# RetNet recurrence and quick-GELU block on one core: decays on GpSimd, four weight loads on GpSimd's queue, keys of step 1 ahead of a weight half, and outputs copied earlier

## The chip, the cores and the metric

The kernel runs on one core of a Trainium2 chip. The metric is the device time of one launch in microseconds (us). A core has five engines that run side by side: PE (matrix products; its weight loads are listed as PEld), DVE (vector), ACT (activation functions and copies), POOL (GpSimd) and SP, which here only issues DMA transfers. Each engine works through its own list of instructions in order, and waits at an instruction until the semaphores it names have been raised by other engines or by transfers that have landed.

## The reference

```python
# attention: q, k, v are (4 batches, 8 heads, 768 positions, 64)
for t in range(S):
    state = gamma * state + k[:, :, t] (outer) v[:, :, t]
    y[:, :, t] = scale * q[:, :, t] @ state
x = y.transpose(0, 2, 1, 3).reshape(3072, 512)
# feed-forward, w_in (512, 2048), w_out (2048, 512)
h = x @ w_in
g = h * (1 / (1 + exp(-1.702 * h)))
out = g @ w_out
```

The attention has one gamma per head and is a recurrence over positions. All inputs but the weights are float32; the two weight matrices reach the kernel as 64-bit floats, that is as pairs of 32-bit words.

## The kernel before, in words

**Attention in steps.** The recurrence is done in chunks of 64 positions, for two batches at a time: 24 steps, numbered j or f. For a step PE turns the queries and keys (`turn_new`, L283), multiplies them within the chunk (`scores`, L339), adds to the state (`gain`, L347), applies the old state (`past`, L358) and the chunk's own scores (`own`, L367). DVE masks the scores (`masked`, L380), scales the share of the old state by the row's decay (`by_state`, "state" in the list, L387), adds both shares into X (`output`, "x" in the list, L409) and adds the gain to the state (`updated`, L432). For step 0 there is no old state, and `output` is a plain copy out of PSUM on ACT (L300, the helper `copy`). `decay` multiplies a step's keys by their column decays: on GpSimd as one instruction over the tile (L318), on ACT as eight instructions, one for each head (L323). `aged` multiplies the state by the decay of a whole chunk (L418 on DVE, L421 on ACT, L423 on POOL).

Scores and gain share one PSUM tile, PAS; past and own share another, PYS. The scores of the next step wait until the state update that reads PAS is done, and past waits until the output copy of the step before has read PYS.

**Weights.** Each pair of 64-bit pieces is fetched by a DMA of 512 KB (`fetch`, L201; `w0a`, `w0b` and so on) into one of three raw places (RAWS: two in W2 and one in G, taken in the order RING), and is narrowed to float32 by six instructions of the class `Narrow`: `abs` (ACT, L237), `low` (ACT, L241), `clip` (DVE, L245), `lift` (DVE, L248), `sign` (DVE, L253), `rest` (DVE, L258). A raw place is free for the next pair when `low` and `sign` of the pair in it are done. Pairs 4 and 7 go to raw places 1 and 2, after pairs 1 and 5.

**Feed-forward.** While weights still arrive, PE multiplies the finished half pieces (`up0` and `up1`, "up" in the list, L476), ACT applies the GELU (`hidden`, "gate", L457), and later units use a product scheme with seven instead of eight products (`zero`, L559, and `seven`, L599), whose sums of weights (`seven_4`, `seven_6`, `seven_52`) and of inputs (`zero_x`, L546) DVE makes. From about 148 us on the down products and the other blocks follow (L954, L698, L821), with the remaining attention steps placed between them.

**What sets the order.** Everything of the first two blocks of four steps is named in one list, written out by hand, at the end of the kernel function. The loop below it calls the works in that order, and their instructions are pinned to it on each engine; `name@engine` gives the engine. So the place of a name in the list sets the place of its instructions in the queue of every engine it uses, and for a load its place in the queue of SP, ACT or POOL:

```python
    for name in """
        row@sp k0@act table q0 v0 z5 rows ...
    """.split():
        name, *e = name.split("@")
        works[name](*[{"sp": sp, "pool": pool, "act": act, "dve": dve}[x] for x in e])
```

A few instructions of `halves_anew` ("anew") are not pinned, and the scheduler places them on POOL: a copy that rewrites `cold` (L1048; it waits until the last decay on ACT has read it), the load of `whole_h` (L1045) and a copy of the mask (L1047).

SP's and ACT's transfers, and POOL's, wait before issue for one of eight landing semaphores of their kind, taken in turn: the ninth transfer waits for the first to land. For steps below 6 the keys come once, by four transfers of 64 KB, and are turned by PE. From step 6 on queries and keys come in squares of 32 (`load`, L176, eight transfers of 32 KB each) that DVE transposes (L294), and the keys come a second time in rows (kn, L161).

Of the kernel before, what the change touches and what calls it, by code (L numbers as in the profile page):

```python
# [28 lines left out]
def kernel(  # L29
# [29 lines left out]
    pe, act, dve, pool, sp = nc.tensor, nc.scalar, nc.vector, nc.gpsimd, nc.sync  # L59
# [42 lines left out]
    rowd = const.tile([P, HP, D], F32, name="rowd")  # L102
    row = G[0:1, 4, 0:2].rearrange("p a (h t) -> p (a h) t", t=D)
    ones = G[0:1, 4, 2, 0:P]
    cold = const.tile([P, 2 * H], F32, name="cold")
    whole = const.tile([P, HP], F32, name="whole")
# [3 lines left out]
    mask = const.tile([P, 2, HP, D], F32, name="mask")  # L110
# [32 lines left out]
    def load(j, what="qkv", engine=None):  # L143

        b, c = j // NC * 2, j % NC
        rows = slice(c * D, (c + 1) * D)
        keep = send if j < 2 * CB else lambda i: i

        def plain(name, src, tag, bufs, engine=sp):
            t = two.tile([P, H, D], F32, name=name + "_in", tag=tag, bufs=bufs)
            QKV[name, j] = t
            for i in range(2):
                if j < NEW:
                    to, at = t[i * D:(i + 1) * D], src[b + i, :, rows, :].rearrange("h p d -> p h d")
                    for n in range(1 if name == "v" else 2):
                        keep(engine.dma_start(*((to, at) if name == "v" else (to[:, n:H:2], at[:, n * HP:(n + 1) * HP]))))
                else:
                    for r in range(2):  # L160
                        keep(engine.dma_start(t[r * D:(r + 1) * D, i * HP:(i + 1) * HP],  # L161
                                              src[b + i, r * HP:(r + 1) * HP, rows, :].rearrange("h p d -> p h d")))

        if j < NEW:
            if "q" in what:
                QKV["q", j] = t = two.tile([P, H * D], F32, name="q_in", tag="q_sq", bufs=2)
                keep((engine or sp).dma_start(t, q[b:b + 2, :, rows, :].rearrange("i h (k p) d -> (i h) k (p d)", p=8)))
            if "k" in what:
                plain("kn", k, "k_sq" if j in (0, 1, 4, 5) else "o", 2, engine or pool)
        elif "q" in what:  # L170
            for name, src in (("q", q), ("k", k)):
                t = two.tile([P, H, D // C4, C4], F32, name=name + "_sq")
                for r0 in range(0, P, C4):
                    for n in range(D // C4):
                        t0 = c * D + n * C4
                        tc.keep_in_program_order(sp.dma_start(  # L176
                            t[r0:r0 + C4, :, n], src[b + r0 // D, :, t0:t0 + C4, r0 % D:r0 % D + C4]
                            .rearrange("h p d -> p h d")))
                QKV[name, j] = t
        if "v" in what:  # L180
            if j >= NEW and c < NC - 1:
                plain("kn", k, "kn", 1)
            plain("v", v, "v", 2, engine or sp)
# [102 lines left out]
    def turn(j):  # L286

        if j < NEW:
            turn_new(j, 1)
            turn_new(j, 0)  # L290
        else:
            QT[j], KT[j] = home(j, "qT"), home(j, "kT")
            for t, name in ((QT[j], "q"), (KT[j], "k")):
                tc.keep_in_program_order(dve.transpose(  # L294
                    t.rearrange("p h t -> p (h t)"), QKV.pop((name, j)).rearrange("p h n d -> p (h n d)")))
        if 2 * CB <= j < NCH - 2:
            load(j + 2, "qk")
# [136 lines left out]
    def step(j, f=None):  # L434
        attend(j, f)
        if j is not None:
            masked(j)
            if j > 2 * CB:
                decay(j)
        if f is not None:  # L440
            c = f % NC
            if c == 0:
                updated(f)
            else:
                by_state(f)
            output(f)
            if 0 < c < NC - 1:
                aged(f)
                updated(f)
        if j is not None and 2 * CB < j < NCH - 1:  # L450
            load(j + 1, "v")
# [587 lines left out]
    def late_loads():  # L1039
        load(2 * CB, "qkv")  # L1040
        load(2 * CB + 1, "qk")
# [61 lines left out]

    begin()
    for name in """
        row@sp k0@act table q0 v0 z5 rows turn_q0 turn_k0 q1 w0b k1@sp w0a mask causal turned_q0
        turned2_q0@dve turned_k0 decay0@pool score0 v1 turn_k1 turn_q1 masked0 gain0 turned_k1 turned_q1 turned2_q1@dve own0 abs0b low0b updated0
        decay1@pool score1 clip0b lift0b sign0b rowd whole q2 k2@sp masked1 abs0a low0a rest0b x0 past1 gain1
        clip0a lift0a sign0a own1 rest0a aged1 turn_k2 turn_q2 w2b w2a state1 updated1 x1 turned_k2 turned_q2 turned2_q2@dve
        v2 q3 k3@sp up0.0.2 score2 abs2 decay2 aged2@dve q4 clip2 lift2 sign2 low2 decay3 w3b w3a  # L1110
        masked2 turn_k3 turn_q3 k4@sp gain2 past2 own2 v3 q5 rest2 k5@sp gate0.0.2 turned_k3 turned_q3 turned2_q3@dve updated2
        state2 score3 decay4 low3 turn_q4 turn_k4 up0.0.3 x2 masked3 gain3 past3 own3 abs3 clip3 lift3 sign3
        turned_q4 turned2_q4@dve rest3 turned_k4 score4 turn_k5 turn_q5 up0.0.6 w1a w5b w1b aged3 updated3 state3 w5a v4
        x3 up0.1.3 turned_q5 turned2_q5@dve gate0.0.3 abs1 low1 abs5 clip1 aged4 lift1 sign1 masked4 own4 gain4 w6a
        rest1 clip5 lift5 gate0.0.6 sign5 up0.0.7 past4 w6b decay5 low5 rest5 updated4 v5 gain5 w4a abs6
        gate0.1.3 turned_k5 clip6 state4 x4 lift6 score5 masked5 w4b abs4 up0.1.7 low6 aged5 gate0.0.7 w7a w7b
        low7 low4 q6 sign6 v6 own5 rest6 past5 seven_4.2 state5 gate0.1.7 seven_6.2 updated5 zero2.0 clip4 up0.1.6
        lift4 sign4 x5 seven_52.2 rest4 turn6 anew decay6 abs7 aged6 up0.1.2 w8a gate0.1.2 clip7 zero_x zero2.1
        score6 past6 q7 w8b v7 zero2.2 masked6 lift7 sign7 gain6 rest7 own6 w11b zero2.3 zero2.4 turn7
        w9a updated6 aged7 gate0.1.6 zero2.5 decay7 zero2.6 state6 w11a seven_4.0 x6 zero0.0 score7 masked7 abs8 clip8  # L1120
        past7 zero0.1 state7 seven_6.0 seven_52.0 lift8 sign8 gain7 own7 x7 seven_x zero0.2 zero0.3 zero0.4 zero0.5 low8
        seven_keep.2 w9b abs9 low11 clip9 rest8 lift9 zero0.6 w10a seven2.0 w10b seven2.1 abs11 clip11 lift11 sign11
        seven_4.1 rest11 seven2.2 abs10 seven2.3 seven2.4 seven_w.1 clip10 lift10 sign9 seven0.0 seven2.5 low10 low9 rest9 sign10
        updated7 rest10 seven_4.3 seven2.6 seven0.1 seven0.2 seven0.3 seven0.4 seven1.0 seven_keep.0 w14b w14a w12b w12a abs12 seven_w.3
        clip12 seven0.5 seven0.6 seven_v.1 lift12 sign12 abs14 clip14 low12 rest12 lift14 sign14 seven1.1 seven1.2 w13a seven1.3
        w13b abs13 low14 seven_v.3 clip13 lift13 seven1.4 sign13 seven3.0 seven1.5 rest14 seven1.6 seven3.1 seven3.2 seven3.3 seven3.4
        w15a seven_keep.3 seven_keep.1 w15b abs15 clip15 lift15 low13 low15 sign15 seven3.5 rest13 seven3.6 rest15 late_loads
    """.split():
        name, *e = name.split("@")
        works[name](*[{"sp": sp, "pool": pool, "act": act, "dve": dve}[x] for x in e])  # L1130
# [109 lines left out]
```

## Time and profile before

| what | value |
|---|---|
| median of the three runs | 650.57 us (649.11, 650.57, 650.80) |
| the profiled execution, its own time | 651.44 us |
| its span, first to last instruction | 649.7 us |
| PE busy | 633.4 us, 97% of the span |
| DVE busy | 435.6 us, 67% |
| ACT busy | 184.4 us, 28% |
| POOL busy | 152.0 us, 23% |
| mean granted clock of PE | 0.997 |
| DMA | 96.86 MB, mean 149 GB/s |
| line with most of PE's time | L821, 840 matmuls of one kind in 100.3 us, 276 ns each |

The page's rows give for a group of instructions the busy time, the mean of one, and the idle time of the engine just before them with what ended it. A row of the timeline gives the start in us from the first instruction, the length, the engine, the line, what is written and read, how many equal instructions are merged, and in brackets the idle time before it and its releaser. Rows of SPq, ACTq and the DMA rows of POOL are issues: the length is that of the issue and not of the transfer.

The profiled execution is one run, and its own time stands 0.87 us above the median; costs are worked out inside it.

### The profile page before, as it was taken

How to read it: one execution, taken by the hardware profiler on the slowest of the kernel's cores; microseconds unless marked ns; L12 is line 12 of the kernel's file. 1: busy time of each engine (PE TensorE's matmuls, PEld its weight loads, DVE VectorE, ACT ScalarE, POOL GpSimd, SP SyncE). 2: the span in 40 equal slices, each digit the busy share in tenths (PEclk: the TensorE clock that was granted, in tenths of full speed). 3: DMA queues.
4: the chain of work that ended last, by engine and by line, in shares of the span. 5: the costliest groups of instructions: out<-in, count | busy, mean ns of one | idle time of the engine just before them, and what ended most of it. 6: DMA issues, size and time to landing. Idle time of an engine off the chain costs nothing.

```text
span 649.7 us, 15510 instructions
## 1 busy us (share of the span) xinstructions
PE 633.4 (97%) x6543; PEld 578.4 (89%) x6543; DVE 435.6 (67%) x643; ACT 184.4 (28%) x329; POOL 152.0 (23%) x184
## 2 busy tenths in 40 slices
PE   7899999999999998999999999999999999999997
PEld 4788888888889997889999889999888999888997
DVE  2879887979989962438874337985246976145854
ACT  3778237661001102332101333100333110233210
POOL 4000211300612435000645000635300425200000
PEclk9989999999999999999999999999999999999999
DMA  9995587783368875720667730667741354221143
GB/s 198 228 258 161 112 252 214 198 209 57 93 200 264 206 175 171 200 67 4 172 179 213 215 85 1 160 161 189 211 95 49 89 174 143 110 91 49 59 153 98
DMA packets 150710, 96.86 MB, mean 149 GB/s; under 512 B 130512, under 2 KB 135888, under 8 KB 149616
## 3 DMA queue, kind: packets, MB, share of 16 engines
q1 hardware_dynamic: 138048, 42.83, 30.2%
q0 software_dynamic: 8672, 40.00, 19.3%
q10 hardware_dynamic: 3920, 13.04, 5.4%
q8 instruction: 51, 0.84, 0.6%
q14 instruction: 19, 0.16, 0.1%
HBM read 79.18 MB, written 14.94 MB: 145 GB/s over the span
## 4 chain that ended last, share of the span: by engine, by line
PE 83%; DMA 9%; SPq 5%; issue 1%; DVE 1%; ACT 1%; ACTq 0%
PE pq L821 33%; PE px L698 17%; PE pz L698 9%; PE pd L954 7%; PE ph L599 6%; PE py L698 4%; DMA W<-in_moe_w_out_dram 2%; SPq L161 2%; PE pa L339 2%; DMA q_in<-in_q_dram 2%; DMA kn_in<-in_k_dram 2%; DMA LATE<-W1D 1%; SPq L176 1%; PE py L367 1%; PE pa L347 1%; DMA v_in<-in_v_dram 1%
## 5 line engine op out<-in xcount | busy, mean ns | idle before, releaser
L821 PE MATMUL pq<-W,G 128*128 128x128 f32 x840 | 100.3, 276 | 0.0
L821 PEld LDWEIGHTS pq<-W,G 128*128 128x128 f32 x840 | 97.0, 192 | 0.8
L796 POOL DMA_DIRECT2D LATE<-W2D x34 | 18.7, 551 | 260.5 <-PE pq L821 139.8
L821 PE MATMUL pq<-LATE 128*128 128x128 f32 x560 | 74.8, 277 | 0.0
L821 PEld LDWEIGHTS pq<-LATE 128*128 128x128 f32 x560 | 68.2, 192 | 0.6
L698 PE MATMUL px<-X,LATE 128*128 128x256 f32 x256 | 60.6, 380 | 2.2 <-DMA LATE<-W1D 2.2
L698 PE MATMUL px<-X,W1A 128*128 128x256 f32 x256 | 60.5, 379 | 0.0
L698 PEld LDWEIGHTS px<-X,LATE 128*128 128x128 f32 x256 | 48.6, 190 | 9.1 <-issue 2.6
L698 PEld LDWEIGHTS px<-X,W1A 128*128 128x128 f32 x256 | 48.4, 190 | 6.3
L743 DVE TENSOR_TENSOR G<-pz,vv 128x512 f32<-128x512 f32 x16 | 11.1, 692 | 51.5 <-ACT vv L713 51.5
L843 ACT ACTIVATE o<-pq 128x512 f32<-128x512 f32 (+1 forms) x18 | 9.8, 544 | 119.9 <-PE pq L821 94.3
L457 ACT ACTIVATE G<-G 128x512 f32<-128x512 f32 x49 | 30.9, 630 | 43.1 <-DVE G L753 19.7
L821 PE MATMUL pq<-LATE,G 128*128 128x128 f32 x280 | 37.0, 275 | 0.0
L821 PE MATMUL pq<-W,LATE 128*128 128x128 f32 x280 | 37.0, 275 | 0.0
L954 PE MATMUL pd<-W,LATE 128*128 128x256 f32 x160 | 35.1, 380 | 0.0
L821 PEld LDWEIGHTS pq<-W,LATE 128*128 128x128 f32 x280 | 34.1, 192 | 0.0
L821 PEld LDWEIGHTS pq<-LATE,G 128*128 128x128 f32 x280 | 34.1, 192 | 0.0
L954 PEld LDWEIGHTS pd<-W,LATE 128*128 128x128 f32 x160 | 30.4, 190 | 4.1
L683 DVE TENSOR_TENSOR G<-G 128x512 f32<-128x512 f32 (+2 forms) x28 | 15.9, 567 | 23.5 <-ACT G L457 23.5
L810 DVE TENSOR_TENSOR LATE<-G 128x512 f32<-128x512 f32 x35 | 27.6, 789 | 5.0 <-PE pq L821 2.2
L476 PE MATMUL ph<-X,W1A 128*128 128x256 f32 x128 | 30.6, 397 | 0.2 <-DVE X L409 0.2
L698 PE MATMUL pz<-X,W1A 128*128 128x256 f32 x128 | 30.3, 380 | 0.0
(214 smaller groups left out, 1163.5 us busy)
## 6 DMA issues: line engine op xcount, KB each, us to landing
LATE<-W2D POOLq DMA_DIRECT2D x34, 768.0 KB, 5.2
W<-in_moe_w_out_dram SPq DMA_DIRECT2D x12, 512.0 KB, 6.0
LATE<-W1D ACTq DMA_DIRECT2D x4, 1536.0 KB, 9.7
LATE<-W1D POOLq DMA_DIRECT2D x4, 1536.0 KB, 8.9
kn_in<-in_k_dram SPq DMA_DIRECT2D x84, 64.0 KB, 4.8
W<-in_moe_w_in_dram SPq DMA_DIRECT2D x10, 512.0 KB, 4.8
out_dram<-o POOLq DMA_DIRECT2D x20, 256.0 KB, 4.6
q_sq<-in_q_dram SPq DMA_DIRECT2D x144, 32.0 KB, 3.0
```

The source lines that it names most:

```text
L161: keep(engine.dma_start(t[r * D:(r + 1) * D, i * HP:(i + 1) * HP], src[b + i, r * HP:(r + 1) * HP, rows, :].rearrange("h p d -> p h d")))
L339: pe.matmul(PAS[HALF[w], u, 0, s, :], kt[HALF[u], w, s, :], qt[HALF[u], w, s, :], start=True, stop=True)
L457: pin(act.activation(g, h[:, i], AF.Gelu_apprx_sigmoid))
L476: pe.matmul(h[:, ab], w, X[:, 2 * th + c // 2, c % 2, :], start=(ab == 0 and c == 0), stop=(c == 3), skip_group_check=True)
L599: pe.matmul(acc[:, u, :], w, x, start=(start and u == 0 and c == 0), stop=(stop and c == 1), skip_group_check=True)
L683: hold(dve.tensor_sub(q[0][1], q[0][0], q[0][1]))
L698: pe.matmul(acc[:, u, :], w1(2 * d + u, sw)[:, c, :], X[:, sx, c, :], start=(start and u == 0 and c == 0), stop=(stop and c == 1), skip_gr ...
L743: dve.tensor_add(a[3], z, v)
L796: engine.dma_start(c, W2D[i])
L810: dve.tensor_add(d[:, 0], s2, a11)
L821: pe.matmul(p0[:, j, :], a[:, d], w[:, d], start=(new and j == 0 and d == 0), stop=(d == NP // 2 - 1), skip_group_check=True)
L954: pe.matmul(p0[:, n, :], g1(m, p, sa)[:, n * P:(n + 1) * P], W2[:, sb, p, :], start=(new and p == 0 and n == 0), stop=(last and p == NP - ...
```

## The change

The list is edited in these places, and `load` lets queries and keys of the late kind be loaded apart:

- `k1@sp`, the four transfers of the keys of step 1, stands ahead of `w0b`, one of the two first weight halves, instead of behind it.
- `x0`, the plain copy of the outputs of step 0 on ACT, stands directly behind `score1` instead of behind `rest0b`; on ACT it passes the copies of the row decays and abs0a and low0a.
- `x1` stands ahead of `updated1`, so that two DVE instructions change places.
- `decay2` and `decay3` are done on POOL, by one instruction each, instead of on ACT by eight each.
- `w4a`, `w4b`, `w7a` and `w7b` are issued by POOL instead of SP.
- `q6` and the new `k6` (and `q7`, `k7`) load queries and keys apart. On SP the issues of q6, k6, the second keys and the values of step 6 keep their order among each other, but now nothing stands between v5 and them.

On POOL the unpinned instructions move too: the copy of `cold` stands between w4 and w7, and the load of `whole_h`, which was issued at 14.30 us, stands behind w7. PE's order does not change.

```diff
-        elif "q" in what:
-            for name, src in (("q", q), ("k", k)):
+        else:
+            for name, src in [(x, y) for x, y in (("q", q), ("k", k)) if x in what]:
...
-        row@sp k0@act table q0 v0 z5 rows turn_q0 turn_k0 q1 w0b k1@sp w0a mask causal turned_q0
+        row@sp k0@act table q0 v0 z5 rows turn_q0 turn_k0 q1 k1@sp w0b w0a mask causal turned_q0
...
-        decay1@pool score1 clip0b lift0b sign0b rowd whole q2 k2@sp masked1 abs0a low0a rest0b x0 past1 gain1
-        clip0a lift0a sign0a own1 rest0a aged1 turn_k2 turn_q2 w2b w2a state1 updated1 x1 turned_k2 turned_q2 turned2_q2@dve
-        v2 q3 k3@sp up0.0.2 score2 abs2 decay2 aged2@dve q4 clip2 lift2 sign2 low2 decay3 w3b w3a
+        decay1@pool score1 x0 clip0b lift0b sign0b rowd whole q2 k2@sp masked1 abs0a low0a rest0b past1 gain1
+        clip0a lift0a sign0a own1 rest0a aged1 turn_k2 turn_q2 w2b w2a state1 x1 updated1 turned_k2 turned_q2 turned2_q2@dve
+        v2 q3 k3@sp up0.0.2 score2 abs2 decay2@pool aged2@dve q4 clip2 lift2 sign2 low2 decay3@pool w3b w3a
...
-        rest1 clip5 lift5 gate0.0.6 sign5 up0.0.7 past4 w6b decay5 low5 rest5 updated4 v5 gain5 w4a abs6
-        gate0.1.3 turned_k5 clip6 state4 x4 lift6 score5 masked5 w4b abs4 up0.1.7 low6 aged5 gate0.0.7 w7a w7b
-        low7 low4 q6 sign6 v6 own5 rest6 past5 seven_4.2 state5 gate0.1.7 seven_6.2 updated5 zero2.0 clip4 up0.1.6
+        rest1 clip5 lift5 gate0.0.6 sign5 up0.0.7 past4 w6b decay5 low5 rest5 updated4 v5 q6 gain5 w4a@pool
+        abs6 gate0.1.3 turned_k5 clip6 state4 x4 lift6 score5 masked5 w4b@pool k6 abs4 up0.1.7 low6 aged5 gate0.0.7
+        w7a@pool w7b@pool low7 low4 sign6 v6 own5 rest6 past5 seven_4.2 state5 gate0.1.7 seven_6.2 updated5 zero2.0 clip4
...
-        score6 past6 q7 w8b v7 zero2.2 masked6 lift7 sign7 gain6 rest7 own6 w11b zero2.3 zero2.4 turn7
+        zero2.1 score6 past6 q7 k7 w8b v7 zero2.2 masked6 lift7 sign7 gain6 rest7 own6 w11b zero2.3
```

(The last lines of the list are only broken elsewhere.)

More of the change, by code (lines that the diff above doesn't have):

```diff
@@ L1114 @@
         x3 up0.1.3 turned_q5 turned2_q5@dve gate0.0.3 abs1 low1 abs5 clip1 aged4 lift1 sign1 masked4 own4 gain4 w6a
-        rest1 clip5 lift5 gate0.0.6 sign5 up0.0.7 past4 w6b decay5 low5 rest5 updated4 v5 gain5 w4a abs6
-        gate0.1.3 turned_k5 clip6 state4 x4 lift6 score5 masked5 w4b abs4 up0.1.7 low6 aged5 gate0.0.7 w7a w7b
-        low7 low4 q6 sign6 v6 own5 rest6 past5 seven_4.2 state5 gate0.1.7 seven_6.2 updated5 zero2.0 clip4 up0.1.6
-        lift4 sign4 x5 seven_52.2 rest4 turn6 anew decay6 abs7 aged6 up0.1.2 w8a gate0.1.2 clip7 zero_x zero2.1
@@ L1119 @@
-        score6 past6 q7 w8b v7 zero2.2 masked6 lift7 sign7 gain6 rest7 own6 w11b zero2.3 zero2.4 turn7
[L1120 to L1127, printed above, removed]
+        rest1 clip5 lift5 gate0.0.6 sign5 up0.0.7 past4 w6b decay5 low5 rest5 updated4 v5 q6 gain5 w4a@pool
@@ new lines @@
+        abs6 gate0.1.3 turned_k5 clip6 state4 x4 lift6 score5 masked5 w4b@pool k6 abs4 up0.1.7 low6 aged5 gate0.0.7
+        w7a@pool w7b@pool low7 low4 sign6 v6 own5 rest6 past5 seven_4.2 state5 gate0.1.7 seven_6.2 updated5 zero2.0 clip4
+        up0.1.6 lift4 sign4 x5 seven_52.2 rest4 turn6 anew decay6 abs7 aged6 up0.1.2 w8a gate0.1.2 clip7 zero_x
+        zero2.1 score6 past6 q7 k7 w8b v7 zero2.2 masked6 lift7 sign7 gain6 rest7 own6 w11b zero2.3
+        zero2.4 turn7 w9a updated6 aged7 gate0.1.6 zero2.5 decay7 zero2.6 state6 w11a seven_4.0 x6 zero0.0 score7 masked7
@@ new lines @@
+        abs8 clip8 past7 zero0.1 state7 seven_6.0 seven_52.0 lift8 sign8 gain7 own7 x7 seven_x zero0.2 zero0.3 zero0.4
+        zero0.5 low8 seven_keep.2 w9b abs9 low11 clip9 rest8 lift9 zero0.6 w10a seven2.0 w10b seven2.1 abs11 clip11
+        lift11 sign11 seven_4.1 rest11 seven2.2 abs10 seven2.3 seven2.4 seven_w.1 clip10 lift10 sign9 seven0.0 seven2.5 low10 low9
+        rest9 sign10 updated7 rest10 seven_4.3 seven2.6 seven0.1 seven0.2 seven0.3 seven0.4 seven1.0 seven_keep.0 w14b w14a w12b w12a
@@ L1128 @@
+        abs12 seven_w.3 clip12 seven0.5 seven0.6 seven_v.1 lift12 sign12 abs14 clip14 low12 rest12 lift14 sign14 seven1.1 seven1.2
+        w13a seven1.3 w13b abs13 low14 seven_v.3 clip13 lift13 seven1.4 sign13 seven3.0 seven1.5 rest14 seven1.6 seven3.1 seven3.2
+        seven3.3 seven3.4 w15a seven_keep.3 seven_keep.1 w15b abs15 clip15 lift15 low13 low15 sign15 seven3.5 rest13 seven3.6 rest15
+        late_loads
     """.split():
```

## The prediction

> **What bounds the kernel now.** I read the page, then the waits and the PE timeline of the first 110 us, then ACT, DVE, POOL and SP in the same stretch, the chain of waits, and the windows with the clock. The page first:
>
> ```profile
> span 649.7 us, 15510 instructions
> PE 633.4 (97%) x6543; PEld 578.4 (89%) x6543; DVE 435.6 (67%) x643; ACT 184.4 (28%) x329; POOL 152.0 (23%) x184
> ```
>
> PE idles for only 16.3 us of the span. By windows 9.1 us of that lies before 40 us, 1.3 us between 60 and 104 us, 5.2 us after 150 us. The change ends its moves by about 90 us, so what it can win is in the first two. The PE timeline of the start (start, length, what, idle before it and what ended it):
>
> ```profile
> 12.20 1.09 PE L283 MATMUL pt<-UB,kn_in 128*128 128x128 f32 x4 [1.38 <-DMA kn_in<-in_k_dram]
> 16.76 1.13 PE L339 MATMUL pa<-G 64*64 64x64 f32 x32 [0.71 <-DVE state L300]
> 18.84 1.13 PE L358 MATMUL py<-G,state 64*64 64x64 f32 x32 [0.95 <-ACT X L300]
> 23.76 4.16 PE L476 MATMUL ph<-X,W1A 128*128 128x256 f32 x16 [0.18 <-DVE X L409]
> 27.85 0.70 PE L339 MATMUL pa<-G 64*64 64x64 f32 x32
> 33.88 0.69 PE L339 MATMUL pa<-G 64*64 64x64 f32 x32 [2.72 <-ACT G L323]
> ```
>
> Two things are to be seen. PE waits in turn for the keys of step 1, for x0 (ACT) and, at 33.88, for the scores of step 3. And the same 32 matmuls take 1.13 us early and 0.70 us from 27.85 on: PE starts at half speed, though the clock column reads 1.00 there. ACT ahead of the 2.72 us hole:
>
> ```profile
> 25.47 2.01 ACT L323 ACTIVATE G<-kn_in,cold 128x64 f32<-128x64 f32 x8
> 27.38 1.18 ACT L241 ACTIVATE W1A<-G 128x1024 f32<-128x1024 uint32 x1
> 28.43 2.04 ACT L323 ACTIVATE G<-kn_in,cold 128x64 f32<-128x64 f32 x8
> 30.34 0.61 ACT L457 ACTIVATE LATE<-ph 128x512 f32<-128x512 f32 x1
> 30.82 1.30 ACT L300 ACTIVATE G<-pt 128x512 f32<-128x512 f32 x3
> ```
>
> ACT is busy without a break from 23.62 to 32.12. Its last row copies the keys and queries of step 3 out of PSUM, 1.3 us after PE had them ready (29.57); DVE's half of the queries ends at 33.02 and its updated2 at 33.74, 0.14 us before PE goes on. So the page's releaser (L323) is only the last thing ACT finished; DVE behind a late ACT is the cause. The windows (PE, PEld, DVE, ACT, POOL busy, then the granted clock) show what the hole costs:
>
> ```profile
> 28.10:31.51 3.41, 3.07 (x136) 2.68 (x127) 2.44 (x4) 3.41 (x12) 0.00 (x0) 1.00 1.21 293
> 31.51:34.93 3.42, 1.04 (x36) 1.01 (x37) 2.70 (x5) 2.68 (x11) 0.00 (x0) 1.00 1.06 177
> 34.93:38.34 3.41, 3.41 (x13) 2.94 (x11) 1.99 (x4) 3.37 (x7) 0.00 (x0) 0.50 0.90 260
> ```
>
> After a stretch with PE 30% busy the next 3.41 us run at half clock. The last place is SP's queue:
>
> ```profile
> 42.35 1.63 SPq L158 DMA_DIRECT2D v_in<-in_v_dram  x2
> 49.19 0.89 SPq L201 DMA_DIRECT2D W<-in_moe_w_in_dram  x2
> 53.71 1.08 SPq L201 DMA_DIRECT2D G<-in_moe_w_in_dram  x2
> 54.84 4.74 SPq L176 DMA_DIRECT2D q_sq<-in_q_dram  x8
> ```
>
> SP stands 5.2 us and 3.6 us before w4 and w7, which wait for DVE's sign1 and sign5, and all later loads stand behind it.
>
> **Part by part.** *Keys of step 1 ahead of w0b.* By the issue and landing record, loads land in the order of issue: q1 9.18, w0b 10.79, k1 11.19 to 12.06, w0a 13.63. Without w0b ahead k1 lands at 9.18 + (12.06 - 10.79) = 10.45; w0b then at 12.06, and its first reader (ACT L237, 15.01) moves up to 13.5, so 1.4 us cover it. PE is free from score0 at about 10.7 instead of waiting to 12.20: **-1.5 us** for all that hangs on k1.
>
> *x0 earlier on ACT.* The wait of 0.95 us before past1 goes; rowd, abs0a and low0a slip 0.6 us. abs0a is then done 1.1 us before DVE's clip0a can take it. Late next is DVE, busy nearly without a break from 15.02 to 23.70, up to x1, for which the first up product (23.76) waits.
>
> *x1 ahead of updated1.* x1 comes 0.6 us earlier; updated1 is first needed by score2 at 27.85, some 4 us later.
>
> *Decays 2 and 3 on POOL.* ACT loses 2.01 + 2.04 us; POOL, idle from 14.9 to 51.2, takes 1.04 us each (L318 rows at 8.82 and 12.22). What the trace does not show is such an operation beside this DVE work. Lower bound 0: beside POOL L423 at 83.82 DVE's L582 took its usual 0.68. Upper bound 1.07: beside POOL L676 DVE's L774 took 1.75 instead of 0.68. Decay 2 can start when k2 has landed (17.62), amid clip0a and lift0a; the nearest row is L245 at 71.29, the same kind as clip0a, which took 1.22 instead of 0.69 and ended 0.55 after POOL's L423, as if it had stood aside until then. I take 1.0, as decay 2 would start just ahead of clip0a. For decay 3 I take 0: DVE then waits for score2.
>
> So the first up product starts at 23.76 - 1.5 - 0.6 + 1.0 = 22.65.
>
> *The clock.* In before full speed begins at 24.69, after a 3.41 us stretch in which PE was 95% busy; earlier stretches, 65 to 86% busy, had not released it. Now 21.28 to 24.69 has a hole (second transposes end at about 21.1, up begins at 22.65), so I take release one stretch later, at 28.10. Sixteen matmuls cost 0.44 us each at half speed and 0.22 at full (7.07 us for 32 at 43.62): 12.3 by 28.10, the rest by 28.9, so score2 comes at 28.9 instead of 27.85, and own2 ends at 32.2. The Trainium skill (TensorE: Matmul & The Clock Gate, part 1) has the same 3.4 us window and calls it free-running; by that the release may fall elsewhere in another run, which one trace cannot show.
>
> *Score3 to score4.* Without decays ACT copies right behind PE: turn_q3 ends at 30.6, ACT at 31.7, DVE's copy and updated2 (0.87 + 0.69) at 33.3: score3 at 33.4 after 1.2 us of hole, PE 65% busy between 31.51 and 34.93. Nothing in the trace lies between 30% (throttled) and 90% (not); I take not throttled, nearer to 90%. Then score3, two transposes and up0.0.3 cost 0.7 + 1.2 + 3.54, gain3, past3 and own3 1.45: score4 at **40.3 instead of 42.11, -1.8**. There is a floor: decay 4 waits for k4 (0.63 us of ACT idle before 32.75), and from it low3, abs3, clip3 to sign3 and the copy of the queries run in a row to 40.72, so score4 could not have come before 40.86. k4 should land about 1 us earlier: q4 ahead of it waited for turn_q2 (22.52 to 23.58, now done by 21.1), the DMA engines were half idle at 24 to 25 us, and whole_h's packets at 17 to 19 us (540 to 650 ns each) move behind w7. Floor 39.8. Ends: -1.25 (k4 unmoved, not counting throttling) and -2.3 (full speed at 24.69).
>
> *40 to 80 us.* From 46.38 to 78.83 DVE is busy 31.71 of 32.45 us; its rest6 ends at 61.54 and PE takes it at 61.67. DVE's run starts with abs1, which follows turned_q5 on ACT, which follows PE's turn_q5 behind score4; so it moves by -1.8 as a whole. w1b (landed 42.16) and w5a (44.59) stay ahead of abs1 and abs5 by 1.2 and 0.9 us.
>
> *w4 and w7 on POOL's queue.* Issued when sign1 and sign5 are done, as before; behind w4 the copy of cold waits for decay 5 (about 49.8), before w7's turn at 51.8, so it holds nothing. whole_h goes out at about 53, needed at 70.92. Landing of 512 KB from POOL is not shown: between 2.2 us (64 KB state copies at 64.65) and 9.48 us (the slowest 512 KB load, 89.87); nearest is 5.2 us for 768 KB (LATE<-W2D). With the new q6 and k6 beside it I take 6: w4 lands at about 53.9, abs4 is due at 53.2. ACT waits 0.7, and low6 behind it has 3.0 us to spare before DVE's rest6. w7's first reader has ACT idle times of 1.7 and 5.8 us behind it. Cost 0.
>
> *SP.* q6, k6, kn6 and v6 go out from about 42 instead of 54.84; behind v5 in the same queue they delay nothing earlier. q7 and k7 are the same 16 issues in the same order. w8a still waits for sign4 (66.7, now 64.9), 5 us before its old turn at 70.31. The chain of waits runs through SP from there to w9b, issued 89.87, landed 99.36, which holds ACT 1.13 us and through it PE 0.61 us at 103.12. With w9b some 4 to 5 us earlier that goes: **-0.6**, between 0 and -0.6.
>
> **Sum**: -1.8 - 0.6 = -2.4 us. The profiled execution took 651.44 (1.74 outside its span), so 649.0; it is 0.87 above the median 650.57. On the median: **648.2**.
>
> **Rivals.**
> 1. *Held by k4 and the clock.* If k4 does not come earlier, score4 stands at its floor of 40.86; and if the unprofiled runs often escape the throttled window already, the win there is only from 40.9 to about 40.3. With the 0.6 at 103.12 half won: about -0.9, **649.7**. For: the floor lies 1.25 us under the old time and DMA engines are full for most of 4 to 47 us. Against: SP's wait for turn_q2 and the idle DMA at 24 us.
> 2. *PE reaches full speed at 24.69 or before.* Score4 at its floor, 39.8: -2.3 - 0.6 = -2.9, **647.7**. Against: the hole after 21.1.
> 3. *Slower: w4 late from POOL's queue.* ACT stops at abs4 in order; from a landing at 56.2 on (53.2 + 3.0, or 8.9 us after issue at 47.3) rest6 is late, DVE has no idle time to give back, and PE's zero2.0 pays one for one. Two pieces of 9.48 us side by side (issues 0.5 us apart) give +1.1, one after the other +10.1; halfway 5.6: 650.57 - 2.4 + 5.6 = **653.8**. For: POOL-issued loads beside busy DVE took 7.9 us (L526, 110.31 to 118.22, an adding transfer). Against: 2.2 us at 64.65, also beside busy DVE. A rule of the Trainium skill speaks for it (SBUF — State Buffer, SBUF: two separate sides): a DMA from GpSimd's queue gets its descriptors written by GpSimd, which is locked out while DVE runs a two-port operation. The 2.2 us row disagrees here.
>
> **How the numbers follow.** Forecast 0.50, rival 1 0.29, rival 2 0.08, rival 3 0.13. A measurement tells about 0.3% (1.95 us) from no change. The forecast lies 0.4 us beyond that line, so a part of it falls inside, and a part of rival 1 outside: faster 0.50, same 0.38, slower 0.12. The range leaves out rival 3 and little else: 646.9 (rival 2 less half a throttled window) to 650.9 (no gain and scatter).
>
> **What would show it.** Transposes of step 1 at about 10.7; no idle before past1; the first up product at 22 to 23; the hole before score3 under 1.5 us and no half clock after 31.5; score4 near 40; zero2.0 near 60; q6 issued before 45; no PE idle near 101. Wrong if a hole and half clock return before 45, if decay 2 costs DVE more than 1.1 us, or if ACT stands at abs4 for over 3 us.

## The result, and the profile after

| | before | after |
|---|---|---|
| median, 22 executions each | 650.60 us (648.50 to 655.58) | **647.56 us** (646.05 to 652.46) |
| ratio of the times, 95% interval | | **0.9951** (0.9937 to 0.9965) |
| the profiled execution, its own time | 651.44 us | 648.59 us |

The change makes the kernel 0.5% faster, about 3.0 us; 2.4 us had been forecast. A second measurement, with the experiments below, gave 0.9972 (0.9953 to 0.9991), so that a gain of 0.6 to 4 us is what can be said. The page of after:

```profile
span 646.9 us, 15504 instructions
PE 631.4 (98%) x6543; PEld 576.1 (89%) x6543; DVE 437.9 (68%) x643; ACT 180.8 (28%) x313; POOL 159.2 (25%) x190
```

ACT lost 3.6 us and POOL gained 7.2. PE's busy time fell by 2.0 us although its 6,543 matmuls are the same: in this execution fewer of them ran at half clock. The PE timeline of the start of after, in the columns of the prediction:

```profile
11.04 1.08 PE L283 MATMUL pt<-UB,kn_in 128*128 128x128 f32 x4 [0.24 <-DMA kn_in<-in_k_dram]
16.09 0.68 PE L358 MATMUL py<-G,state 64*64 64x64 f32 x32
17.75 1.11 PE L347 MATMUL pa<-v_in,G 64*64 64x64 f32 x32 [0.99 <-issue]
22.78 3.72 PE L476 MATMUL ph<-X,W1A 128*128 128x256 f32 x16 [1.28 <-DVE X L409]
26.43 0.69 PE L339 MATMUL pa<-G 64*64 64x64 f32 x32
31.94 0.69 PE L339 MATMUL pa<-G 64*64 64x64 f32 x32 [1.15 <-DVE state L432]
38.94 1.05 PE L339 MATMUL pa<-G 64*64 64x64 f32 x32 [0.27 <-DVE G L300]
```

The first up product (22.78) now waits 1.28 us for DVE's x1: DVE is what is late there. One wait is new: 0.99 us before gain1 (17.75), which starts right behind DVE's masked1 (16.97 to 17.65). The three waits named in the prediction have changed as it said: the one for the keys of step 1 is 0.24 us instead of 1.38, the one for x0 is gone (16.09), the one before score3 is 1.15 us instead of 2.72 and names DVE's updated2. Score4 starts at 38.94 instead of 42.11. The windows of after with the clock (PE, PEld, DVE, ACT, POOL busy, then the granted clock):

```profile
11.00:14.42 3.42, 3.38 (x64) 3.08 (x68) 1.15 (x3) 1.95 (x4) 2.09 (x3) 1.00 1.19 289
14.42:17.83 3.41, 1.55 (x88) 1.33 (x84) 3.31 (x8) 3.04 (x7) 0.00 (x0) 1.00 1.16 236
17.83:21.24 3.41, 3.41 (x72) 3.27 (x72) 3.21 (x6) 1.66 (x5) 1.23 (x1) 0.50 1.18 286
28.07:31.48 3.41, 1.70 (x97) 1.52 (x96) 3.32 (x6) 1.00 (x4) 0.00 (x0) 1.00 1.39 185
```

Full speed came at 14.42 already, behind a stretch with PE 99% busy, was lost for one window after a stretch with PE 45% busy, and from 21.24 on stayed until PE was done, although the stretch from 28.07 was only 50% busy. The last place is SP's queue and the wait behind it. SP of after:

```profile
44.92 6.80 SPq L176 DMA_DIRECT2D q_sq<-in_q_dram  x8
51.76 7.04 SPq L176 DMA_DIRECT2D k_sq<-in_k_dram  x8
...
85.61 0.58 SPq L201 DMA_DIRECT2D W<-in_moe_w_out_dram  x1
```

q6 goes out 9.9 us earlier, but its 16 squares need 13.9 us instead of 10.0 (SP waits for landing semaphores), and w8a behind them still waits for DVE's sign4, which ends at 65.22. So w8a goes out 5.0 us earlier (65.29 instead of 70.31), and w9b (85.61) 4.3 us earlier; it lands at 94.70 instead of 99.36. In before ACT stood for w9b and PE behind ACT:

```profile
98.89 3.62 PE L599 MATMUL ph<-W,W1A 128*128 128x256 f32 x16
99.38 1.14 ACT L237 ACTIVATE G<-W 128x1024 f32<-128x1024 f32 x1 [1.13 <-DMA W<-in_moe_w_out_dram]
103.12 5.23 PE L599 MATMUL ph<-x,w 128*128 128x256 f32 x23 [0.61 <-ACT p L604]
```

In after PE does not wait there:

```profile
97.61 3.62 PE L599 MATMUL ph<-W,W1A 128*128 128x256 f32 x16
101.06 1.24 PE L599 MATMUL ph<-x,w 128*128 128x256 f32 x5
```

### The profile page after: what moved, and what is told of

It reads as the page before. It is cut to its first block, busy times and chain, and to the rows that moved or that the text cites. A ratio compares the mean times of both kernels' runs of the same rounds, so it can differ in the third digit from the quotient of the medians.

```text
span 646.9 us, 15504 instructions
## 1 busy us (share of the span) xinstructions
PE 631.4 (98%) x6543; PEld 576.1 (89%) x6543; DVE 437.9 (68%) x643; ACT 180.8 (28%) x313; POOL 159.2 (25%) x190
## 4 chain that ended last, share of the span: by engine, by line
PE 87%; DMA 6%; DVE 2%; SPq 1%; ACT 1%; issue 1%; ACTq 0%; DVEq 0%
PE pq L821 34%; PE px L698 17%; PE pz L698 9%; PE pd L954 8%; PE ph L599 5%; PE py L698 4%; PE ph L559 3%; PE pa L339 2%; DMA W<-in_moe_w_in_dram 2%; PE py L367 1%; DMA kn_in<-in_k_dram 1%; PE pa L347 1%; PE py L599 1%; PE py L358 1%; DMA q_sq<-in_q_dram 1%; DMA W1A<-W1A 1%
## 5 line engine op out<-in xcount | busy, mean ns | idle before, releaser
L698 PE MATMUL py<-X,W1A 128*128 128x256 f32 x128 | 30.2, 379 | 0.0
```

Of the source, the lines that this page charges most:

```text
L698: pe.matmul(acc[:, u, :], w1(2 * d + u, sw)[:, c, :], X[:, sx, c, :], start=(start and u == 0 and c == 0), stop=(stop and c == 1), skip_gr ...
```

## The experiments

**Theory A**: the win is made in the first 40 us (keys, x0, decays). **Theory B**: it is made by SP's queue, free of w4 and w7; what the early parts win is lost later on. All ratios are to before, timed on the same chip in the same series.

| kernel | median | before | ratio, 95% interval |
|---|---|---|---|
| p_k1 | 649.62 | 650.35 | 0.9994 (0.9976 to 1.0013) |
| p_x | 649.38 | 650.35 | 0.9992 (0.9977 to 1.0007) |
| p_decay | 650.15 | 650.35 | 0.9999 (0.9980 to 1.0017) |
| p_loads | 647.96 | 650.35 | 0.9966 (0.9950 to 0.9983) |
| abc | 649.62 | 649.61 | 1.0000 (0.9979 to 1.0021) |
| abc_w9 | 647.95 | 649.61 | 0.9970 (0.9954 to 0.9985) |
| whole_late | 649.42 | 649.61 | 0.9994 (0.9977 to 1.0010) |
| loads_wh | 648.02 | 649.61 | 0.9968 (0.9953 to 0.9984) |
| abc_again | 649.71 | 650.40 | 0.9984 (0.9962 to 1.0006) |
| after_again | 649.30 | 650.40 | 0.9972 (0.9953 to 0.9991) |
| loads_again | 648.71 | 650.40 | 0.9969 (0.9950 to 0.9989) |
| all_but_decays | 647.09 | 650.40 | 0.9939 (0.9912 to 0.9967) |

From the traces, the starts of five PE instructions that all kernels share (in before: score4 42.11, zero2.0 61.67, the first L559 behind zero_x 73.89, the first L599 98.89, and the first L599 behind ACT's L604 103.12) and w9b's landing. The sixteen matmuls of L599 take 3.45 us until the next starts wherever PE does not wait, so the last column is the fifth start less the fourth less 3.45 (0.17 us more than the bracket of a row, which counts from a modelled end):

| trace | score4 | zero2.0 | 73.89 | 98.89 | 103.12 | w9b landed | PE waits |
|---|---|---|---|---|---|---|---|
| before | 42.11 | 61.67 | 73.89 | 98.89 | 103.12 | 99.36 | 0.78 |
| p_k1 | 41.40 | 60.95 | 73.53 | 99.14 | 103.01 | 99.27 | 0.42 |
| p_x | 39.11 | 59.19 | 72.43 | 97.97 | 103.01 | 99.27 | 1.59 |
| p_decay | 40.51 | 60.68 | 73.62 | 98.98 | 103.23 | 99.47 | 0.80 |
| whole_late | 40.15 | 60.49 | 73.19 | 98.17 | 102.77 | 99.00 | 1.15 |
| abc | 39.03 | 59.22 | 71.55 | 96.55 | 100.40 | 96.65 | 0.40 |
| abc_again | 38.68 | 58.86 | 71.43 | 96.41 | 100.68 | 96.92 | 0.82 |
| abc_w9 | 40.30 | 60.48 | 73.43 | 98.62 | 102.07 | 93.37 | 0 |
| p_loads | 39.76 | 59.71 | 72.36 | 97.33 | 100.78 | 94.28 | 0 |
| loads_wh | 42.07 | 61.63 | 73.88 | 98.85 | 102.30 | 95.93 | 0 |
| loads_again | 42.12 | 61.67 | 73.93 | 98.90 | 102.35 | 95.60 | 0 |
| after | 38.94 | 60.08 | 72.64 | 97.61 | 101.06 | 94.70 | 0 |
| after_again | 39.25 | 59.52 | 71.86 | 96.84 | 100.29 | 95.29 | 0 |
| all_but_decays | 40.58 | 60.53 | 72.83 | 97.82 | 101.27 | 95.96 | 0 |

### The four parts, each alone

p_k1 moves only the keys, p_x only the outputs of steps 0 and 1, p_decay only the decays, p_loads only the loads:

```diff
- q1 w0b k1@sp w0a
+ q1 k1@sp w0b w0a
...
- score1 clip0b ... rest0b x0 past1 ... state1 updated1 x1
+ score1 x0 clip0b ... rest0b past1 ... state1 x1 updated1
...
- decay2 ... decay3
+ decay2@pool ... decay3@pool
...
- v5 gain5 w4a ... w4b abs4 ... w7a w7b low7 low4 q6 ... q7
+ v5 q6 gain5 w4a@pool ... w4b@pool k6 abs4 ... w7a@pool w7b@pool low7 low4 ... q7 k7
```

> The kernel before with one part alone: the four key transfers of step 1 ahead of w0b. Theory A (the win is made in the first 40 us, by PE starting earlier and by ACT losing the decays): first transposes of step 1 at 11.0 instead of 12.2, first up product about 1.1 us earlier, but decays 2 and 3 still fill ACT, so a hole of 2 us or more before the scores of step 3 stays; in all -0.3 to -1.0 us. Theory B (the win is made by SP's queue being free from 44 us on; what is won in the first 40 us is lost in DVE's full stretch from 45 to 78 us): 0.

> The kernel before with x0 directly behind the scores of step 1 and x1 ahead of updated1, and nothing else. Theory A: the 0.95 us wait before past1 goes and the first up product comes 0.6 us earlier, of which the ACT-made hole before the scores of step 3 takes most: -0.6 to 0. Theory B: 0.

> The kernel before with decays 2 and 3 on POOL and nothing else. Theory A: the hole before the scores of step 3 shrinks from 2.7 to under 1.7 us, no half clock from 34.9 to 38.3, scores of step 4 about 1 to 1.5 us earlier; in all -0.8 to -1.5, the largest of the early parts. DVE loses 0.7 to 1.0 us once to POOL's decay 2. Theory B: 0 to -0.3.

> The kernel before with w4 and w7 on POOL's queue and queries and keys of steps 6 and 7 loaded early, and nothing else. Theory A: nothing changes before 50 us; the 0.6 us wait at 103 goes, and the wait for W1D at 257 (2.2 us before, 0.8 in the changed kernel) shrinks if it hangs on SP's queue; -0.6 to -2.0. Theory B: most of the whole, -2 to -3.

Measured: the loads alone make 0.9966, the other three nothing that can be told from no change. Theory A falls as it stands, although in the traces each early part did what was expected of it: in p_k1 the transposes came at 11.06 and the first up product at 22.65, in p_x the wait before past1 is gone and the up product came at 23.00, in p_decay the hole before score3 is 1.15 us and score4 came at 40.51. p_x shows where an early gain goes. Its PE is 1.46 us ahead at 73.89, still 0.92 at 98.89, and 0.11 us ahead at 103.12. About half a microsecond of it is lost near 85 us, where DVE stands 0.90 us for the keys' squares of step 7 (81.48) and PE 0.33 us behind DVE (85.31). The other 0.81 us is lost at 103. PE and ACT of p_x there:

```profile
97.97 3.62 PE L599 MATMUL ph<-W,W1A 128*128 128x256 f32 x16
103.01 0.48 PE L599 MATMUL ph<-x,w 128*128 128x256 f32 x1 [1.42 <-ACT p L604]
```
```profile
99.30 1.13 ACT L237 ACTIVATE G<-W 128x1024 f32<-128x1024 f32 x1 [2.11 <-DMA W<-in_moe_w_out_dram]
...
102.36 0.59 ACT L604 ACTIVATE p<-ph 128x512 f32<-128x512 f32 x1
```

ACT stands 2.11 us for w9b (abs9, 99.30), works through low11 and two gates, and only then makes the copy p that PE waits for. The row of PE names ACT; what it waits for is a load. I call this the **wall**: while w9b lands at 99.0 to 99.5, the product behind p starts at 102.8 to 103.2, however early PE is.

### The three early parts together, and w9b moved without POOL

abc is p_k1, p_x and p_decay together, with the loads as in before; abc_w9 is abc with this besides:

```diff
- w9a ... w11a ... seven_keep.2 w9b
+ w9a w9b ... w11a ... seven_keep.2
```

> The kernel before with three of the four parts of the change: keys of step 1 ahead of w0b, x0 and x1 earlier, decays 2 and 3 on POOL; the four weight loads and q6 stay where they were. Wall theory: until about 100 us PE runs 1.5 to 2.5 us ahead of before, but w9b still goes out near 90 us on SP's queue, so that the first product of L599 behind ACT L604 starts at 102.8 to 103.2 as in before (103.12), with PE idle 1.5 to 2.5 us there; time 649.5 to 650.4, ratio 0.998 to 1.000. Theory that the early parts add up: that product starts at 101.0 to 101.6; time 647.5 to 648.5, ratio 0.996 to 0.997.

> The same three parts, and on SP w9b directly behind w9a instead of behind w11a and the three saves of seven_keep.2; nothing is moved to POOL. Wall theory: w9b is issued about 2 us earlier and lands 2 us earlier, so the wall stands at about 101.0 to 101.4 instead of 103.1, and the time is 1.5 to 2 us below that of the kernel with the three parts alone (648 to 648.8, ratio 0.9965 to 0.998). Theory that the win needs the weight loads of pairs 4 and 7 on POOL for another reason (the early part of the run, DMA traffic): no difference to the three parts alone, within 0.5 us.

Measured: abc is as slow as before (1.0000), abc_w9 1.67 us faster than abc. Both ratios are the wall theory's; that the early parts add up (0.996 to 0.997) is refuted for abc. w9b moved up on SP (issued 87.48 and landed 93.37, against 89.87 and 99.36 in before) is enough, with no load on POOL. In its one trace PE does not wait; it comes to the product only at 102.07, later than the 101.0 to 101.4 of the theory; that execution kept half speed until 27.67, and its score4 was already 1.27 us behind that of abc. The trace of abc, though, is not what the theory expected: w9b landed at 96.65 and PE reached the product at 100.40. That execution took 646.40 us, the fastest of its twelve, so abc was run again:

> The same kernel as abc once more, for a second trace and twelve more times: the first trace was the fastest of its twelve executions (646.40 us against a median of 649.62). Wall theory: a usual execution has w9b issued at 89 to 90 us and landed at 99.0 to 99.5, PE idle 0.6 to 2.5 us between 98 and 110 us, the product of L599 behind ACT L604 at 102.7 to 103.2; median within 0.7 us of the kernel before. Theory that there is no wall and the first trace is the usual one: that product at 100 to 101 and little idle; median 2 us below the kernel before.

Measured: again no gain in the median that can be told (0.9984, though this interval, 0.9962 to 1.0006, would allow 0.997), and again the profiled execution is the fastest of its twelve (646.75), with w9b landed at 96.92. Half of the expectation missed: the wall is not fixed at 103. It moves with SP's queue: in abc the second eight squares of step 6 went out from 58.03 and w9b at 86.93, in p_x, with q6 only 0.96 us later than in abc, from 59.84 and at 89.74. PE still waits 0.4 and 0.8 us behind it. Why the other executions of abc are 3 us slower than the two in the traces has not been seen.

### The side effect: whole_h

In p_loads and in after the load of whole_h leaves at 53 to 54 us instead of 14.30, out of the crowded start. The first kernel does only this; the second is p_loads with whole_h early again:

```diff
+        pin(pool.tensor_copy(cold[HALF[1], H:H + HP], cold[HALF[1], H + HP:2 * H]))
         pin(pool.dma_start(whole_h, ...
...
-        pool.tensor_copy(cold[HALF[1], H:H + HP], cold[HALF[1], H + HP:2 * H])
...
-        decay1@pool score1 ... rowd whole q2
+        decay1@pool score1 ... rowd whole whole_h q2
```

> The kernel before with only one thing changed: the load of whole_h on POOL stands behind the copy of cold, so that it goes out at about 51 us instead of 14.3 us, as it does in the changed kernel. Theory that this side effect (no packets of whole_h among the loads of 15 to 30 us) makes the win of the load part: time 648 to 648.6, ratio 0.9965 to 0.9975, keys of step 4 land 0.5 to 1 us earlier. Wall theory: ratio 0.9995 to 1.0005, 650.1 to 650.6.

> The load part alone (w4 and w7 on POOL, q6 and k6 behind v5), but whole_h issued early again, behind the loads of whole at about 14 us, as in before. Wall theory: as the load part alone, ratio 0.9960 to 0.9975, 648 to 648.7, L599 at 100.8 to 101.3. Theory that whole_h makes the win: ratio 0.999 to 1.000.

Measured: 0.9994 and 0.9968. The side effect is worth nothing that can be told from no change, and the load part wins as much without it. So its win is in w4, w7 and the squares; these were not tried apart from each other.

### The whole, the loads and all but the decays in one series

```diff
all_but_decays
-        score2 abs2 decay2@pool ... low2 decay3@pool
+        score2 abs2 decay2 ... low2 decay3
```

> The changed kernel once more, for a second trace and for times on the same chip as the next two. Ratio to before 0.994 to 0.997; in the trace w9b issued by 87 us, landed by 96, and no idle time of PE between 98 and 110 us, wherever the half clock falls at the start.

> The load part alone once more, beside the whole change. Theory that the early parts count once the queue of SP is free: the whole change is 0.8 to 1.8 us faster than this. Theory that they are lost anyway, in DVE's full stretch or in the wait for pair 4: the two agree within 0.5 us.

> The whole change without its third part: decays 2 and 3 stay on ACT, eight instructions each. Theory that the decays on POOL win (4.05 us less on ACT, 1.5 us more on DVE, a smaller hole before score3): this is 0.5 to 1.2 us slower than the whole change, and the hole before score3 is above 2 us. Theory that POOL's share of DVE's time takes the win away: equal within 0.4 us, or faster.

Measured: whole 0.9972, loads 0.9969, all but the decays 0.9939. after_again lies a hair outside its range, its w9b (issued 85.28, landed 95.29) and PE's missing wait inside. That the early parts add 0.8 to 1.8 us to the loads is not borne out here. By the first measurement of after (0.9951) against the three of the load part (0.9966 to 0.9969) they would add about 1 us; by this series nothing. That the decays on POOL win is not borne out either: without them the hole before score3 was 3.06 us, as expected, and score4 came at 40.58 instead of 39.25, yet this is the fastest kernel of the series, 2.2 us below the whole. Its interval, from eight executions, overlaps with both of the whole change, so it is not shown to beat after.

The trace of loads_again is a clean cut, because its clock fell as in before's trace: to within 0.05 us PE does the same up to 98.90, and then

```profile
98.90 3.62 PE L599 MATMUL ph<-W,W1A 128*128 128x256 f32 x16
102.35 1.03 PE L599 MATMUL ph<-x,w 128*128 128x256 f32 x4
```

against 103.12 in before. The load part alone takes away 0.77 us here, and nothing ahead of it. loads_wh, whose clock fell the same way too, says the same: 98.85, then 102.30. From before to loads_again the span shrinks by 1.85 us; 0.85 of the rest lies between this product and PE's end, most of it in waits that change from execution to execution (before 2.21 us at 257, loads_again 0.79 at 214 and 0.65 at 445), and 0.23 behind PE's end.

## Why the prediction was right, and where it was not

The total was right for a reason that was half wrong. The prediction put -1.8 us into the first 40 us and -0.6 into SP's queue; the runs put all that can be told from no change into the queue. That the one error made up for the other is luck: the load part alone, at 0.9966 to 0.9969, would have come nearer to the forecast of 648.2 (648.4 to 648.6) than the whole change did. Nor does the total choose between the forecast and rival 2: the measured 647.56 lies on rival 2's 647.7, and its condition, full speed at 24.69 or before, is what both traces of after show; it had been given 0.08.

The traces of after, taken alone, would have confirmed the sum: the product of 103.12 comes 2.06 and 2.83 us earlier, 0.78 of it PE's lost wait and 1.28 and 2.05 won ahead of it. But p_loads, with none of the early parts, has it 2.34 us earlier as well, because its full speed came at 16.83. One trace each cannot tell the early parts from the clock's draw.

- **Keys of step 1**, -1.5: the transposes came at 11.04 and, in after_again, 10.76: -1.2 and -1.4. k1 landed at 10.90 instead of the 10.45 worked out. Right.
- **x0 and x1**: the wait before past1 is gone. Right, but 0.99 us of waiting now stand one step on, before gain1.
- **Decays on POOL**, decay 2 at 1.0 and decay 3 at 0: DVE's sign0a and sign2 paid. DVE and POOL of after:

```profile
19.08 1.49 DVE L253 SCALAR_TENSOR_TENSOR W1A<-W,W1A 128x256 uint32<-128x256 uint32 x2
```
```profile
18.71 1.23 POOL L318 TENSOR_TENSOR G<-kn_in,cold 128x512 f32<-128x512 f32 x1 [5.57 <-DMA kn_in<-in_k_dram]
```

The pair took 0.76 us in before: 0.73 us for decay 2, and the same for decay 3 (2.02 instead of 1.29). The sum for both was 1.0, measured 1.46. The first up product came at 22.78 and 22.62, against 22.65.
- **The clock**, release at 28.10: the step that failed. It came at 14.42 in after and 13.50 in after_again, each time with one half-speed window later on, and score2 came at 26.43 and 27.95 instead of 28.9. A hole and half clock before 45, which the prediction had named as a sign of being wrong, did come. The prediction looked only at the stretch that had released the clock in before, 21.28 to 24.69, and not at what the change does to the stretches ahead of it. Before, p_decay and after happen to have their 3.41 us windows in the same place to 0.03 us; PE is 66% and 50% busy from 11.0 to 14.4 in the first two, which released at 24.69 and 24.66, and 99% in after. The prediction's own numbers had this: the transposes at 10.7 and the 3.9 us of matmuls behind them fill 11.03 to 14.45. Where the windows fall counts as well. Of the seven traces with the keys of step 1 early six release between 12.53 and 14.88 and one at 27.67; of the other seven two release at 15.64 and 16.83, five between 21.61 and 24.84. The sentence on the Trainium skill (TensorE: Matmul & The Clock Gate, part 1) that calls the window free-running should have carried this part of the step. The traces agree that it is: the windows lie anywhere against the first instruction. They do not agree with the 0.5 us either way by which, the section says, the transition varies. That a stretch 65% busy is not throttled was right. That nothing in before's trace lies between 30 and 90% was a misreading: from 253.42 to 256.84 PE is 42% busy, and no half clock follows.
- **Score4**, 40.3 with a floor of 39.8: it came at 38.94 and 39.25. The floor took the copy of the queries to its end (39.26 in after: 38.37 and 0.89), but PE starts before it ends, at about the end of its first half. k4 moved up as expected: decay 4 starts at 31.48 instead of 32.75, with

```profile
31.48 2.02 ACT L323 ACTIVATE G<-kn_in,cold 128x64 f32<-128x64 f32 x8 [2.38 <-DMA kn_in<-in_k_dram]
```

so ACT now waits 2.38 us for rival 1's k4, and through low3, abs3 to sign3 and that copy score4 waits for it too (0.27 us of PE before 38.94).
- **40 to 80 us**: the gain was to pass on in full. Of 3.17 us at score4 1.59 was left at zero2.0 (60.08) in after; in after_again 2.15 of 2.86. Too hopeful as a rule; the 1.8 us forecast for this place lies between the two.
- **w4 on POOL**, landing 6 us after issue, ACT waiting 0.7 of 3.0 us of cover: the second piece landed 7.35 us after its issue (after_again 6.94), and ACT waited

```profile
56.33 1.17 ACT L237 ACTIVATE G<-W 128x1024 f32<-128x1024 f32 x1 [2.71 <-DMA W<-in_moe_w_in_dram]
```

2.71 us. The cost is 0, as taken, with 0.26 us to spare (low6 ends at 58.55, rest6 starts at 58.81): a landing 0.3 us later would have begun to cost, so rival 3 was near. In loads_again ACT waited 1.37 us for w4 and 3.01 for w7, and PE lost nothing up to 98.90.
- **SP**, -0.6: q6 issued before 45 (44.92), no PE idle near 101, w9b 4.3 us earlier: right. The size is the mis-sized term: 0.77 us in the clean cut, but 1.6 to 2.4 us in the medians of the load part. What it left out is that waits for SP's loads also eat what was won ahead of them (p_x 1.35 of 1.46 us, 0.81 of it at the wall), and by the medians of p_k1, p_x, p_decay and abc the early parts bring nothing without the load part.

**Open.** The traces show 0.4 to 1.6 us of PE waiting at the wall; the medians give the load part 1.6 to 2.4 us and abc_w9 over abc 1.7. Where the rest lies in executions that were not profiled is not settled. A small piece is at the end: from PE's last matmul to the last instruction it is 3.71 to 3.73 us in the eight traces without the load part and 3.49 to 3.50 in the six with it; why was not looked into. before's trace also has a PE wait of 2.21 us at 257 us for a late load of LATE, of which the other thirteen show 0 to 0.8; whether usual executions of before have it was not tried, and it is not counted to the change.

## What to carry to other kernels

A gain is worth what reaches the next place where a fixed queue of loads ends last: read, behind the stretch you speed up, which DMA wait stands next, and whether that load's issue moves with your gain. An engine named as the releaser may itself be standing behind a load; follow the wait one instruction further. A single trace of a kernel with a 3.41 us clock window is one draw: before costing a step by the clock, ask what another phase would give, and which earlier stretch the change itself fills.

## What was not expected of the hardware

- **Clock.** Over fourteen traces, in the first 40 us and by windows of 3.41 us: nine stretches with PE 21 to 46% busy were each followed by a window at half clock, twenty stretches at full speed with 47 to 66% were not, and one with 56% was (PE's busy time by its matmul rows). The share alone does not settle it: before's stretch from 253.42, 42% busy, was not followed by half clock either. The first release followed stretches 87 to 100% busy, but one with 90% did not release (17.43 in abc_w9), and neither did six of 90 to 100% that began within the first 2.3 us.
- **DVE beside POOL.** A decay on POOL mostly held up the DVE instruction that it met by 0.73 to 0.87 us: the pair of two-input instructions (L253) for both decays in after, after_again, abc and abc_again and for decay 3 in abc_w9; elsewhere a one-input L245, from 0.42 to 1.26 us in abc_w9 and from 0.69 to 1.53 in p_decay. The first decay of p_decay cost least: L258 took 0.93 instead of 0.69. The Trainium skill (SBUF — State Buffer, SBUF: two separate sides) gives the shared ports, for the whole instruction, to whichever of POOL's instruction and a DVE one with two inputs from SBUF, or in a two-port mode, starts first; the traces agree: in after decay 2 started at 18.71 and ended at 19.94, and the pair that came at 19.08 took 0.73 us longer.
- **Weight loads on POOL's queue** beside a busy DVE and SP's squares landed 4.4 to 8.6 us after issue, 512 KB each, over the six traces that have them; the prediction's 6 is inside, its bound of 9.48 was not reached.
